# Eleven block units in each of the last two quarters, with the S sums and the den chain moved

## The chip, the cores and the metric

The kernel runs on one core of a Trainium2 chip. The metric is the device time in microseconds of one execution. A core has a matrix engine (TensorE, "PE" in the profile; its weight loads are "PEld"), a vector engine (VectorE, "DVE"), a scalar engine (ScalarE, "ACT"), GpSimd ("POOL"), and a queue engine (SyncE, "SP") that issues most of the transfers. Each engine works through its own list of instructions in order and waits for the others where data or a buffer demands it. TensorE writes into PSUM, which has eight banks of 128 x 512 float32; this kernel cuts the eight banks up by hand.

## The reference

Two branches over the same 2048 tokens of 640 features are blended by a gate.

```python
def _A_ref(x, wqkv, wo):                     # linear attention, 32 heads of 20
    ...
    phi = lambda t: jnp.where(t > 0, t + 1, jnp.exp(t)) + 1e-6
    pq, pk = phi(q), phi(k)
    kv = jnp.einsum("bhsd,bhse->bhde", pk, v)
    z = jnp.einsum("bhsd->bhd", pk)
    num = jnp.einsum("bhqd,bhde->bhqe", pq, kv)
    den = jnp.einsum("bhqd,bhd->bhq", pq, z)[..., None] + 1e-6
    o = num / den
    return (...)(o).reshape(B, S, D) @ wo

def _B_ref(x, w_gate, w_up, w_down):         # 640 -> 1728 -> 640
    return (_gelu(x @ w_gate) * (x @ w_up)) @ w_down

g = _sigmoid((x * gate_w).sum(-1, keepdims=True))
return g * a + (1 - g) * b
```

## The kernel before

The tokens are cut into four quarters of 512, and each quarter into four tiles of 128 (tile 0 to 15). On TensorE the stages follow one another like this (starts of the matmuls in the trace):

| stage | from, us | what |
|---|---|---|
| start, E(0) | 0 | keys and queries of quarter 0, then gate and up of quarter 0 |
| KQ | 44 | keys and queries of quarters 1 to 3 |
| G | 81 | the product of tokens and keys that kv is made of |
| E(1) | 96.7 | gate and up of quarter 1; beside it KV, M and the sums for the down weights |
| F(0) | 128.5 | down of quarter 0, together with its attention part, and the blend |
| E(2) | 146.6 | gate and up of quarter 2 |
| F(1) | 174.1 | |
| E(3) | 192.4 | |
| F(2) | 219.4 | |
| F(3) | 237.5 | down of quarter 3, and the last rows of the output |

**E(q).** The 1728 hidden features are 13 tiles of 128 ("F tiles", `ft`) and half a tile. For one F tile a *plain unit* does gate and up with five 512-column matmuls each. A *block unit* does the same with a 2x2 block scheme of seven products in place of eight: four blocks of gate and up weights (two k tiles each) against four blocks of x (two k tiles by 256 tokens). Each product is two 256-column matmuls; the fifth k tile stays plain, one 512-column matmul each for gate and up. The scheme needs sums of weights (made once by GpSimd in E(0), kept in DRAM as `stash`, fetched again for each block unit of E(2) and E(3)) and sums of x (`tx`, made by VectorE for each quarter).

```python
    WF = tuple(range(4, 12)) + (2, 3)          # F tiles that have weight sums
    ...
    def unit(q, ft, of=UB, ahead=(0, 0)):      # plain
        ...
            return lambda: nc.tensor.matmul(ps, lhsT=w[:, k, f * P : (f + 1) * P], rhs=xT[q][:, k, :],
                                            start=(k == 0), stop=(k == ND - 1))
    ...
    def unit_b(q, ft, fetch):                  # block: p1 to p7 are the seven products
        ...
        def p5():
            two(ub[:, hi_h], s_(1), tx[0], True)
        def p1():
            two(ub[:, lo_h], wg[:, 0:2, fs], X[:, 0:2, lo_h])
            nc.scalar.copy(out=gb[:, lo_h], in_=ub[:, lo_h])
            nc.scalar.copy(out=cp, in_=ub[:, hi_h])
        ...
        def p3():
            nc.vector.tensor_tensor(out=ub[:, hi_h], in0=ub[:, hi_h], in1=c3, op=ALU.add)
            two(gb[:, hi_h], s_(4), X[:, 2:4, hi_h])
            w_fetch(*fetch)                    # sums of the unit five places on
        def g5():
            mm(gb, wg[:, 4, fs], X[:, 4, :])
        ...
        return [p5, p1], [p6], [p7, p3, g5, p2], [u5, p4]
    ...
    runs = {
        0: blocks([3], 12, range(4, 12), [NF - 1]),
        1: list(range(1, NF)),
        2: blocks([NF - 1, 1, 12], 0, range(2, 12), [None]),
        3: blocks([1, 12], 0, range(2, 12), [NF - 1]),
    }
```

A unit ends with a gelu on ScalarE (`gl`) and a product on VectorE, which empties the bank of the up half (line 250, written to `hb` or `hT`).

**F(q).** Down is a block scheme of the same kind, once for each half `a` of the tiles. It needs sums of the weights (`TS`, "T sums") and of the hidden activations (`SS`, "S sums" s1 to s4, each in three parts: h, p and x). `keep` and `join` empty the banks; `beside` puts other work at that place of the order.

```python
        for a in range(2):
            st = [4 * q + 2 * i + a for i in range(2)]
            beside("F", q, a)
            ...
            product(x, a, 0, 0, 0, 0, 0, 0, True, True)
            c1 = keep("c1", x, 0)                       # ScalarE
            product(b11, a, 0, 0, 1, 0, 1, 0, not a, bool(a))
            ...
            product(x, a, 2, 0, 0, 2, 0, 0, False, True)    # needs s2
            c2 = keep("c2", x, 0)
            product(b22, a, 1, 0, 0, 1, 0, 0, not a, True)  # needs s1
            join(d[:], b22, 0, c2)                      # VectorE, the "d join"
            beside("D", q, a)
            product(x, a, 3, 0, 0, 3, 0, 0, False, True)    # needs s3
            c3 = keep("c3", x, 1)
            product(b12, a, 4, 0, 0, 0, 1, 1, not a, bool(a))   # needs s4
            if not a:
                ...
                join(o[0][:, 0:HALF], b11, 0, c1)       # its bank is x of the next half
            join(o[0][:, HALF:D], b12, 0, d)
            dma(out=out2[st[0] * P : (st[0] + 1) * P, :], in_=o[0][:])
            join(o[1][:, HALF:D], b22, 1, c3)
            product(b21, a, 0, 1, 1, 4, 0, 0, False, True)
            join(o[1][:, 0:HALF], b21, 1, c3)
            dma(out=out2[st[1] * P : (st[1] + 1) * P, :], in_=o[1][:])
```

**The den chain.** For each pair of token tiles: `den_mul` (GpSimd: `prod` = pq x zrep), `den_sum` (VectorE: the sum over a head), `den_rec` (GpSimd: `dtmp`), `den_inv2` (VectorE: reciprocal `rg`), `den_out` (GpSimd: pq x rg), `den_turn` (a transposing transfer into `pqT`, which F(q) reads). `den_inv` is den_sum twice, den_rec and den_inv2. Where each piece stands is fixed by a table; its part around F(0):

```python
        (1, 9): [(phase_S, 0, "h", 0)],
        (1, 10): [(phase_S, 0, "p", 0)],
        (1, 11): [(phase_S, 0, "x", 0)],
        (1, 12): [(den_mul, 4, 5)],
        ("F", 0, 0): [(w_fetch, (2, 2), (2, 3), (2, 4)), (phase_S, 0, "h", 1)],
        ("D", 0, 0): [(phase_S, 0, "p", 1), (phase_S, 0, "x", 1)],
        ("F", 0, 1): [(h_twin, 1), (x_tiles,), (t_sums, 2), (den_inv, 4), (den_mul, 6, 7), (den_out, 4, 5)],
        ("D", 0, 1): [(den_inv, 6), (den_out, 6, 7)],
        (2, 0): [(ring_more,), (w_fetch, (2, 5), (2, 6)), (s_tiles, 1), (den_mul, 8, 9), *s_pool(1, 0)],
```

A key `(q, n)` stands after the unit n of E(q), `("F", q, a)` and `("D", q, a)` at the two `beside` calls above.

Of the kernel before, what the change touches and what calls it, by code (L numbers as in the profile page):

```python
# [9 lines left out]
ALU = mybir.AluOpType  # L10
AX = mybir.AxisListType
FP32 = mybir.dt.float32
# [4 lines left out]
def kernel(  # L17
# [12 lines left out]
    nc = tc.nc  # L30
# [71 lines left out]
    x_sb = [x_all[:, 4 * q : 4 * q + 4, :] for q in range(NQ)]  # L102
    WF = tuple(range(4, 12)) + (2, 3)
    WS = 2 * 4
    ws = [ov.tile([P, 2, WS, P], FP16, name=f"ws{i}", tag="slab_a", bufs=NQ) for i in range(3)]
    ws.append(ov.tile([P, 2, WS, P], FP16, name="ws3", tag="slab_g"))
    pk_q = []
# [162 lines left out]

    ws.append(ew["more"])
    stash = dram.tile([len(WF), P, WS, P], FP16, name="stash")

    def w_sums(i):

        n = 2
# [15 lines left out]

    def t_sums(q):

        def blk(k, j):
            return xT[q][:, 2 * k : 2 * k + 2, j * HT : (j + 1) * HT]

        t1, t2, t3, t4 = ew["tx"]
        for out, a0, a1 in ((t1, blk(0, 1), blk(0, 0)), (t2, blk(1, 1), t1), (t3, blk(1, 1), blk(0, 1)),
                            (t4, blk(1, 0), t2)):  # L300
            sums(out, a0, a1, ALU.subtract)

# [423 lines left out]

    def den_inv2(st):
        rg = work.tile([P, 2, H, 1], FP32, name="rg", bufs=2)
        nc.vector.reciprocal(out=rg[:, :, :, 0], in_=den_at[st, "t"][:])
        dn[st], dn[st + 1] = rg[:, 0], rg[:, 1]  # L730
# [74 lines left out]
    def phase_F(q):  # L805
# [35 lines left out]
        for a in range(2):  # L841
# [53 lines left out]
            dma(out=out2[st[1] * P : (st[1] + 1) * P, :], in_=o[1][:])  # L895

    def blocks(first, ramp, fs, last):
# [61 lines left out]
    with tc.manual_schedule(engines={mybir.EngineType.PE, mybir.EngineType.Activation, mybir.EngineType.DVE}):  # L959
# [12 lines left out]
        (0, 4): [(w_sums, 3)],  # L972
        (0, 6): [(w_sums, 4)],
        ("K", 4): [(x_sums, 3)],
    })
# [33 lines left out]
    def s_tiles(q):  # L1009
        if q == 0:  # L1010
            sw = ov.tile([P, NG * D], FP16, name="sw", tag="slab_w")
            sp = ov.tile([P, ND * D], FP16, name="sp", tag="slab_g")
            SS["3"], SS["4"] = (t[:, 0 : KS * TW].rearrange("p (k n) -> p k n", n=TW) for t in (sw, sp))
            SS["more"] = sp[:, KS * TW : KS * TW + WS // 2 * P].rearrange("p (s c) -> p s c", c=P)
            SS["c1"] = sw[:, KS * TW : KS * TW + 4 * HALF].bitcast(FP32).rearrange("p (s n) -> p s n", n=HALF)
        for i in range(1, 5):
            name = f"s{q}_{i}"
            if q == NQ - 1:
                SS[q, i] = big.tile([P, KS, TW], FP16, name=name, tag="pq" if i < 4 else "xT", bufs=NQ if i < 4 else NQ - 1)
            elif i < 3:  # L1020
                SS[q, i] = ov.tile([P, KS, TW], FP16, name=name, tag="slab_a", bufs=NQ)
            else:
                SS[q, i] = SS[str(i)]

    def t_tiles():
        TS[2] = ov.tile([P, KS, HALF], FP16, name="t2", tag="slab_e")
# [3 lines left out]

    def s_pool(q, a):
        return [(phase_S, q, part, a, (3, 1, 2, 4), nc.gpsimd) for part in "hpx"]

    side.update({
        (1, 1): [(m_part, 0), (t_tiles,), (den_mul, 0, 1, 2, 3)],
        (1, 2): [(m_part, 1), (den_inv, 0), (den_out, 0, 1)],
        (1, 3): [(den_inv, 2), (den_out, 2, 3)],
        (1, 4): [(s_tiles, 0), (h_twin, 0), (phase_T, "h", (1,))],
        (1, 5): [(phase_T, "h", (3, 2))],
        (1, 6): [(phase_T, "x", (1, 3))],  # L1040
        (1, 7): [(phase_T, "h", (4,)), (phase_T, "x", (2, 4))],
        (1, 8): [(phase_T, "p", (1, 2, 3, 4))],
        (1, 9): [(phase_S, 0, "h", 0)],
        (1, 10): [(phase_S, 0, "p", 0)],
        (1, 11): [(phase_S, 0, "x", 0)],
        (1, 12): [(den_mul, 4, 5)],
        ("F", 0, 0): [(w_fetch, (2, 2), (2, 3), (2, 4)), (phase_S, 0, "h", 1)],
        ("D", 0, 0): [(phase_S, 0, "p", 1), (phase_S, 0, "x", 1)],
        ("F", 0, 1): [(h_twin, 1), (x_tiles,), (t_sums, 2), (den_inv, 4), (den_mul, 6, 7), (den_out, 4, 5)],
        ("D", 0, 1): [(den_inv, 6), (den_out, 6, 7)],  # L1050
        (2, 0): [(ring_more,), (w_fetch, (2, 5), (2, 6)), (s_tiles, 1), (den_mul, 8, 9), *s_pool(1, 0)],
        (2, 7): [(den_rec, 8), *s_pool(1, 1)],
        (2, 10): [(den_inv2, 8), (lambda: den_out(8, 9, later=True),)],
        ("F", 1, 0): [(den_turn, 8, 9)],
        ("D", 1, 0): [(t_sums, 3), (lambda: pool_hold(ew["tx"][3][:, 0, 0:1]),), (den_mul, 10, 11)],
        ("F", 1, 1): [(h_twin, 2), (den_inv, 10), (den_mul, 12, 13), (den_out, 10, 11)],
        ("D", 1, 1): [(den_inv, 12), (den_mul, 14, 15), (den_out, 12, 13)],
        (3, 0): [(s_tiles, 2), (den_sum, 14, 0), (den_sum, 14, 1), (den_rec, 14), *s_pool(2, 0)],
        (3, 2): [(den_inv2, 14), (lambda: den_out(14, 15, later=True),), *s_pool(2, 1)],
        (3, 11): [(den_turn, 14, 15)],  # L1060
        ("D", 2, 0): [(s_tiles, 3)],
# [4 lines left out]
    })  # L1066
    for n in range(4):
        side[2, 3 + n] = [(den_sum, 8, n // 2, slice(H // 2 * (n % 2), H // 2 * (n % 2 + 1)))]
# [35 lines left out]
```

## Time and profile before

| | before |
|---|---|
| time, median of 3 | 261.82 us (261.49 to 262.46) |
| span of the profiled execution | 259.3 us |
| matmuls | 1755 |
| TensorE clock granted | full |
| GpSimd busy | 135.2 us (52%) |

A profile line of the timeline gives start, duration, engine, source line, operation, what is written and read, its shape, and how many like instructions are merged in it; in brackets stands idle time ahead of it and what ended it. A line of the waits gives who waited for whom, the sum in us, how often, and the longest. Two things are needed for reading TensorE here. First, the end of a matmul is modelled and overlaps the next one, so that a hole of a few tenths is not always shown as idle; the distance from start to start is the sure measure. Second, a wait is charged to the instruction that released it, which may itself have been ready long before and merely have stood behind others in its engine's list.

### The profile page before, as it was taken

Reading aid. Unit: us, or ns where it says so; the run is one execution under the profiler, and the core shown is the slowest. Engines: PE = TensorE matmul, PEld = TensorE weight load, DVE = VectorE, ACT = ScalarE, POOL = GpSimd, SP = SyncE. Lnnn points to the kernel's source line nnn. Section 1 sums busy time; section 2 is a strip of 40 time slices with the busy share of each in tenths; the row PEclk is TensorE's granted clock in tenths of the full one; section 3 lists DMA queues with packets and bytes.
Section 4 is the critical chain, followed back from the end, with each engine's and each line's share of the span. In section 5 each row is a group of like instructions: output and inputs, shape, how many; then the busy total and the mean of one; then the engine's idle time right before and its main releaser. Section 6 shows DMA issues by size and latency. Waiting matters only on the chain.

```text
span 259.3 us, 4883 instructions
## 1 busy us (share of the span) xinstructions
PE 253.8 (98%) x1755; PEld 160.9 (62%) x1755; DVE 183.7 (71%) x366; ACT 121.8 (47%) x271; POOL 135.2 (52%) x158
## 2 busy tenths in 40 slices
PE   8999999999999999999999999999999999999994
PEld 3655686555556775444466647777666787767672
DVE  0698577778779995679999567784756777268632
ACT  3689677555555234732231147762224876311110
POOL 6109995255550004785000999997799999400000
PEclk9999999999999999999999999999999999999999
DMA  7999999900000029125041157441223531011011
GB/s 234 319 350 237 168 357 263 378 4 0 1 3 0 1 41 317 53 68 109 0 125 51 25 129 216 132 142 26 78 51 83 162 93 22 0 52 53 0 51 52
DMA packets 42164, 28.82 MB, mean 111 GB/s; under 512 B 21532, under 2 KB 40860, under 8 KB 42140
## 3 DMA queue, kind: packets, MB, share of 16 engines
q1 hardware_dynamic: 41698, 28.03, 38.5%
q10 hardware_dynamic: 442, 0.49, 0.6%
q8 instruction: 13, 0.21, 0.4%
q14 instruction: 11, 0.09, 0.1%
HBM read 17.86 MB, written 5.24 MB: 89 GB/s over the span
## 4 chain that ended last, share of the span: by engine, by line
PE 88%; DVE 5%; POOL 2%; DMA 2%; issue 1%; SPq 0%; DVEq 0%
PE banks L320 21%; PE banks L827 20%; PE banks L443 17%; PE banks L240 14%; PE banks L330 7%; PE banks L546 6%; DMA wqk<-in_A_wqkv_dram 2%; PE banks L536 2%; DVE o_out L853 1%; POOL prod L709 1%; POOL pq_93 L744 1%; PE banks L834 1%; DVE den L717 1%; DVE tx L61 1%; DVE hb L250 1%
## 5 line engine op out<-in xcount | busy, mean ns | idle before, releaser
L245 ACT ACTIVATE gl<-banks 128x512 bf16<-128x512 f32 x52 | 31.0, 598 | 31.6 <-PE banks L240 17.1
L462 ACT ACTIVATE phi<-banks 128x512 bf16<-128x512 f32 (+1 forms) x36 | 18.8, 526 | 16.2 <-POOL hold L799 8.9
L250 DVE SCALAR_TENSOR_TENSOR hb<-banks,gl 128x512 bf16<-128x512 f32 x26 | 17.8, 683 | 8.4 <-PE banks L320 2.8
L849 ACT ACTIVATE m_all<-banks,omg_s 128x320 f32<-128x320 f32 x16 | 8.4, 527 | 31.6 <-PE banks L827 31.6
L250 DVE SCALAR_TENSOR_TENSOR hT_152<-banks,gl 128x512 bf16<-128x512 f32 x26 | 17.9, 689 | 7.2 <-PE banks L320 4.8
L724 POOL TENSOR_SCALAR dtmp<-den,en_s 128x32 f32<-128x32 f32 x16 | 4.6, 291 | 24.5 <-DVE den L717 23.5
L320 PEld LDWEIGHTS <-wg 128*128 128x128 bf16 x140 | 13.7, 98 | 5.2
L384 DVE TENSOR_TENSOR banks<-banks,zacc 128x256 f32<-128x256 f32 x28 | 12.1, 431 | 6.0 <-ACT zacc L381 3.8
L240 PE MATMUL banks<-xT_89,wg 128*128 128x512 bf16 x65 | 16.2, 379 | 0.0
L240 PE MATMUL banks<-xT_89,wu 128*128 128x512 bf16 x65 | 16.1, 379 | 0.0
L799 POOL CAST hold<-phi 128x1 f32<-128x1 bf16 x12 | 2.2, 183 | 24.6 <-DVE phi L464 24.6
L853 DVE SCALAR_TENSOR_TENSOR o_out<-banks,omg_s,m_all 128x320 bf16<-128x320 f32 x24 | 12.0, 537 | 3.1 <-PE banks L827 3.1
L853 DVE SCALAR_TENSOR_TENSOR m_all<-banks,omg_s,m_all 128x320 f32<-128x320 f32 x8 | 4.4, 550 | 13.2 <-PE banks L827 13.2
L240 PEld LDWEIGHTS <-wu 128*128 128x128 bf16 x80 | 7.8, 98 | 9.4
L381 ACT COPY zacc<-banks 128x256 f32<-128x256 f32 x28 | 10.4, 370 | 6.6 <-PE banks L320 6.5
L849 ACT ACTIVATE sw<-banks,omg_s 128x320 f32<-128x320 f32 x8 | 4.2, 527 | 19.5 <-PE banks L827 19.5
L240 PEld LDWEIGHTS <-wg 128*128 128x128 bf16 x80 | 7.5, 98 | 8.4 <-issue 0.5
L443 PE MATMUL banks<-wqk,xT_88 128*128 128x512 bf16 (+2 forms) x80 | 12.2, 299 | 0.4 <-DMA wqk<-in_A_wqkv_dram 0.4
L709 POOL TENSOR_TENSOR prod<-pq_92,zrep 128x640 f32<-128x640 bf16 x2 | 2.8, 1408 | 18.6 <-ACT zrep L617 18.6
L717 DVE TENSOR_REDUCE den<-prod 128x32 f32<-128x640 f32 (+1 forms) x16 | 11.2, 726 | 0.7 <-POOL prod L709 0.5
L443 PE MATMUL banks<-wqk,xT_89 128*128 128x512 bf16 (+1 forms) x60 | 11.6, 344 | 0.0
L320 PE MATMUL banks<-tx,wr 128*128 128x256 f16 x64 | 11.6, 273 | 0.0
(291 smaller groups left out, 693.1 us busy)
## 6 DMA issues: line engine op xcount, KB each, us to landing
wr<-stash SPq DMA_DIRECT2D x20, 128.0 KB, 2.7
out_dram<-o_out SPq DMA_DIRECT2D x16, 160.0 KB, 1.8
wd<-in_B_w_down_dram SPq DMA_DIRECT2D x1, 2080.0 KB, 9.0
wr_1729<-stash SPq DMA_DIRECT2D x16, 128.0 KB, 2.1
x_all<-in_A_x_dram SPq DMA_DIRECT2D x3, 640.0 KB, 5.7
wqk<-in_A_wqkv_dram SPq DMA_DIRECT2D x1, 800.0 KB
wg<-in_B_w_gate_dram SPq DMA_DIRECT2D x1, 800.0 KB, 9.1
wu<-in_B_w_up_dram SPq DMA_DIRECT2D x1, 800.0 KB
```

What stands on the lines that cost most here:

```text
L240: nc.tensor.matmul(ps[:, t0 : t0 + tw], lhsT=w[:, dk, ft * P : (ft + 1) * P], rhs=xT[q][:, dk, t0 : t0 + tw], start=(dk == 0), stop=(dk == ...
L245: nc.scalar.activation(out=gl[:], in_=psg[:], func=ACT.Gelu_apprx_tanh)
L250: nc.vector.scalar_tensor_tensor(out=hT_cur[q][:, ft, :], in0=psu[:], scalar=HS, in1=gl[:], op0=ALU.mult, op1=ALU.mult)
L320: nc.tensor.matmul(out, lhsT=lhsT, rhs=rhs, start=start, stop=True, skip_group_check=True)
L330: return lambda: nc.tensor.matmul(ps, lhsT=w[:, k, f * P : (f + 1) * P], rhs=xT[q][:, k, :], start=(k == 0), stop=(k == ND - 1))
L443: nc.tensor.matmul(ps[:, 0 : hi - lo], lhsT=xT[q][:, dk, sl * P : (sl + 1) * P], rhs=wqk[:, dk, lo:hi], start=(dk == 0), stop=(dk == ND - 1),)
L462: nc.scalar.activation(out=e[:, lo:top], in_=ps[:, lo:top], func=ACT.Exp)
L546: nc.tensor.matmul(bank[:, 0:HALF], lhsT=lhsT, rhs=rhs, start=(start and n == 0), stop=(stop and n == NG2 - 1), skip_group_check=True)
L717: nc.vector.tensor_reduce(out=den_at[st][:, i, hs], in_=dn[st + i][:].rearrange("p (h c) -> p h c", c=Dh)[:, hs], axis=AX.X, op=ALU.add)
L827: nc.tensor.matmul(bank[:, 0:HALF], lhsT=lhs(sa, ia, ka * KS + kk, a), rhs=rhs(sb, kb * KS + kk, jb), start=(start and kk == 0), stop=(sto ...
L849: nc.scalar.activation(out=c[:], in_=bank[:, 0:HALF], func=ACT.Copy, scale=omg[i])
L853: nc.vector.scalar_tensor_tensor(out=out, in0=bank[:, 0:HALF], scalar=omg[i], in1=c[:], op0=ALU.mult, op1=ALU.add)
```

## The change

It turns F tile 1 into a block unit in E(2) and E(3), so that eleven F tiles of each are block units; for that, one more set of weight sums is made in E(0). It makes the S sums of F(0) earlier, in one piece for both halves, over E(1), so that F(0) has none beside it. With that, it moves the den chain of tiles 4 to 7 and of 12 to 15 to other places: `den_rec` of a pair comes ahead of the outputs of the pair before, and the reciprocal of tiles 8, 9 and 14, 15 comes in two pieces beside later units. A `hold` on GpSimd keeps the den products of tiles 4 and 5 behind the last S sum. The last row of tiles is stored in two halves, the first as soon as it is ready. The core of the diff:

```diff
-    WF = tuple(range(4, 12)) + (2, 3)
+    WF = tuple(range(4, 12)) + (2, 3, 1)
...
-    ws.append(ov.tile([P, 2, WS, P], FP16, name="ws3", tag="slab_g"))
+    ws3 = ov.tile([P, 3, WS, P], FP16, name="ws3", tag="slab_g")
+    ws.append(ws3[:, 0:2])
...
-    ws.append(ew["more"])
+    ws += [ew["more"], ws3[:, 2:3]]
...
-    def den_inv2(st):
-        rg = work.tile([P, 2, H, 1], FP32, name="rg", bufs=2)
-        nc.vector.reciprocal(out=rg[:, :, :, 0], in_=den_at[st, "t"][:])
+    def den_inv2(st, pair=slice(0, 2)):
+        if (st, "r") not in den_at:
+            den_at[st, "r"] = work.tile([P, 2, H, 1], FP32, name="rg", bufs=2)
+        rg = den_at[st, "r"]
+        nc.vector.reciprocal(out=rg[:, pair, :, 0], in_=den_at[st, "t"][:, pair])
...
+            end = q == NQ - 1 and a
...
             join(o[1][:, HALF:D], b22, 1, c3)
+            row = out2[st[1] * P : (st[1] + 1) * P, :]
+            if end:
+                dma(out=row[:, HALF:D], in_=o[1][:, HALF:D])
             product(b21, a, 0, 1, 1, 4, 0, 0, False, True)
             join(o[1][:, 0:HALF], b21, 1, c3)
-            dma(out=out2[st[1] * P : (st[1] + 1) * P, :], in_=o[1][:])
+            dma(out=row[:, 0:HALF] if end else row, in_=o[1][:, 0:HALF] if end else o[1][:])
...
-        2: blocks([NF - 1, 1, 12], 0, range(2, 12), [None]),
-        3: blocks([1, 12], 0, range(2, 12), [NF - 1]),
+        2: blocks([NF - 1, 12], 0, range(1, 12), [None]),
+        3: blocks([12], 0, range(1, 12), [NF - 1]),
...
+        (0, 7): [(w_sums, 5)],
...
+        ("S", 0): [(s_tiles, 0), (phase_S, 0, "h", None, (1,))],
+        ("S", 1): [(phase_S, 0, "h", None, (2,))],
...
-        (1, 6): [(phase_T, "x", (1, 3))],
+        (1, 6): [(phase_S, 0, "h", None, (3, 4)), (phase_T, "x", (1, 3))],
...
-        (1, 9): [(phase_S, 0, "h", 0)],
-        (1, 10): [(phase_S, 0, "p", 0)],
-        (1, 11): [(phase_S, 0, "x", 0)],
-        (1, 12): [(den_mul, 4, 5)],
-        ("F", 0, 0): [(w_fetch, (2, 2), (2, 3), (2, 4)), (phase_S, 0, "h", 1)],
-        ("D", 0, 0): [(phase_S, 0, "p", 1), (phase_S, 0, "x", 1)],
-        ("F", 0, 1): [(h_twin, 1), (x_tiles,), (t_sums, 2), (den_inv, 4), (den_mul, 6, 7), (den_out, 4, 5)],
-        ("D", 0, 1): [(den_inv, 6), (den_out, 6, 7)],
-        (2, 0): [(ring_more,), (w_fetch, (2, 5), (2, 6)), (s_tiles, 1), (den_mul, 8, 9), *s_pool(1, 0)],
+        (1, 9): [(phase_S, 0, "p")],
+        (1, 10): [(phase_S, 0, "x")],
+        (1, 12): [(lambda: pool_hold(SS[0, 4][:, KS - 1, 0:1]),), (den_mul, 4, 5)],
+        ("F", 0, 0): [(x_tiles,), (t_sums, 2), (w_fetch, (2, 1), (2, 2), (2, 3))],
+        ("D", 0, 0): [(den_inv, 4), (den_mul, 6, 7)],
+        ("F", 0, 1): [(h_twin, 1), (den_sum, 6, 0), (den_sum, 6, 1), (den_rec, 6), (den_out, 4, 5)],
+        ("D", 0, 1): [(den_inv2, 6), (den_out, 6, 7)],
+        (2, 0): [(ring_more,), (w_fetch, (2, 4), (2, 5)), (s_tiles, 1), (den_mul, 8, 9), *s_pool(1, 0)],
...
-        (2, 10): [(den_inv2, 8), (lambda: den_out(8, 9, later=True),)],
+        (2, 9): [(den_inv2, 8, slice(0, 1))],
+        (2, 10): [(den_inv2, 8, slice(1, 2)), (lambda: den_out(8, 9, later=True),)],
...
-        ("F", 1, 1): [(h_twin, 2), (den_inv, 10), (den_mul, 12, 13), (den_out, 10, 11)],
-        ("D", 1, 1): [(den_inv, 12), (den_mul, 14, 15), (den_out, 12, 13)],
-        (3, 0): [(s_tiles, 2), (den_sum, 14, 0), (den_sum, 14, 1), (den_rec, 14), *s_pool(2, 0)],
-        (3, 2): [(den_inv2, 14), (lambda: den_out(14, 15, later=True),), *s_pool(2, 1)],
-        (3, 11): [(den_turn, 14, 15)],
+        ("F", 1, 1): [(h_twin, 2), (den_inv, 10), (den_mul, 12, 13)],
+        ("D", 1, 1): [(den_sum, 12, 0), (den_sum, 12, 1), (den_rec, 12), (den_out, 10, 11), (den_mul, 14, 15)],
+        (3, 0): [(s_tiles, 2), (den_inv2, 12), (den_out, 12, 13), *s_pool(2, 0)],
+        (3, 7): [(den_rec, 14), *s_pool(2, 1)],
+        (3, 9): [(den_inv2, 14, slice(0, 1))],
+        (3, 10): [(den_inv2, 14, slice(1, 2)), (lambda: den_out(14, 15, later=True),)],
+        ("F", 2, 0): [(den_turn, 14, 15)],
...
     with tc.manual_schedule():
+        beside("S", 0)
         phase_E(1, 0)
+        beside("S", 1)
```

More of the change, by code (lines that the diff above doesn't have):

```diff
@@ L269, in phase_E @@
             e_half(q, pgu)
-    ws.append(ew["more"])
+    ws += [ew["more"], ws3[:, 2:3]]
     stash = dram.tile([len(WF), P, WS, P], FP16, name="stash")
     def w_sums(i):
-        n = 2
+        n = len(WF[2 * i : 2 * i + 2])
         f0 = WF[2 * i] * P
@@ L291, in w_stash, with t_sums @@
             dma(out=stash[2 * i + f], in_=ws[i][:, f])
-    def t_sums(q):
+    def t_sums(q, eng=nc.vector):
         def blk(k, j):
@@ L300, in t_sums @@
                             (t4, blk(1, 0), t2)):
-            sums(out, a0, a1, ALU.subtract)
+            sums(out, a0, a1, ALU.subtract, eng)
     def w_fetch(*keys, eng=dma):
@@ L1010, in s_tiles @@
         if q == 0:
-            sw = ov.tile([P, NG * D], FP16, name="sw", tag="slab_w")
             sp = ov.tile([P, ND * D], FP16, name="sp", tag="slab_g")
-            SS["3"], SS["4"] = (t[:, 0 : KS * TW].rearrange("p (k n) -> p k n", n=TW) for t in (sw, sp))
+            SS["4"] = sp[:, 0 : KS * TW].rearrange("p (k n) -> p k n", n=TW)
             SS["more"] = sp[:, KS * TW : KS * TW + WS // 2 * P].rearrange("p (s c) -> p s c", c=P)
-            SS["c1"] = sw[:, KS * TW : KS * TW + 4 * HALF].bitcast(FP32).rearrange("p (s n) -> p s n", n=HALF)
-        for i in range(1, 5):
+        for i in (1, 2, 4) if q == 0 else range(1, 5):
             name = f"s{q}_{i}"
@@ L1023, in s_tiles, with s3_tile @@
                 SS[q, i] = SS[str(i)]
+    def s3_tile():
+        sw = ov.tile([P, NG * D], FP16, name="sw", tag="slab_w")
+        SS["3"] = SS[0, 3] = sw[:, 0 : KS * TW].rearrange("p (k n) -> p k n", n=TW)
+        SS["c1"] = sw[:, KS * TW : KS * TW + 4 * HALF].bitcast(FP32).rearrange("p (s n) -> p s n", n=HALF)
     def t_tiles():
@@ L1029, in m_part, with s_pool @@
         phase_M(((0, 0), (0, 1), (1, 0)) if i == 0 else ((1, 1), (2, 0), (2, 1)))
-    def s_pool(q, a):
-        return [(phase_S, q, part, a, (3, 1, 2, 4), nc.gpsimd) for part in "hpx"]
+    def s_pool(q, a, parts="hpx"):
+        return [(phase_S, q, part, a, (3, 1, 2, 4), nc.gpsimd) for part in parts]
     side.update({
+        ("S", 0): [(s_tiles, 0), (phase_S, 0, "h", None, (1,))],
+        ("S", 1): [(phase_S, 0, "h", None, (2,))],
         (1, 1): [(m_part, 0), (t_tiles,), (den_mul, 0, 1, 2, 3)],
@@ L1037 @@
         (1, 3): [(den_inv, 2), (den_out, 2, 3)],
-        (1, 4): [(s_tiles, 0), (h_twin, 0), (phase_T, "h", (1,))],
+        (1, 4): [(s3_tile,), (h_twin, 0), (phase_T, "h", (1,))],
         (1, 5): [(phase_T, "h", (3, 2))],
-        (1, 6): [(phase_T, "x", (1, 3))],
+        (1, 6): [(phase_S, 0, "h", None, (3, 4)), (phase_T, "x", (1, 3))],
         (1, 7): [(phase_T, "h", (4,)), (phase_T, "x", (2, 4))],
         (1, 8): [(phase_T, "p", (1, 2, 3, 4))],
-        (1, 9): [(phase_S, 0, "h", 0)],
@@ L1066 @@
     })
-    for n in range(4):
-        side[2, 3 + n] = [(den_sum, 8, n // 2, slice(H // 2 * (n % 2), H // 2 * (n % 2 + 1)))]
+    for q, st in ((2, 8), (3, 14)):
+        for n in range(4):
+            side[q, 3 + n] = [(den_sum, st, n // 2, slice(H // 2 * (n % 2), H // 2 * (n % 2 + 1)))]
     with tc.manual_schedule():
+        beside("S", 0)
         phase_E(1, 0)
+        beside("S", 1)
         phase_KV()
```

## The prediction

> **What bounds the kernel now.** I read the page first (busy shares, then the slices, then the chain), after that the waits of TensorE, and last the timelines around each place where TensorE stood still.
>
> ```profile
> PE 253.8 (98%) x1755; PEld 160.9 (62%) x1755; DVE 183.7 (71%) x366; ACT 121.8 (47%) x271; POOL 135.2 (52%) x158
> ...
> PE 88%; DVE 5%; POOL 2%; DMA 2%; issue 1%; SPq 0%; DVEq 0%
> ```
>
> TensorE is the bound from end to end: busy 98% of 259.3 us, at full clock. A shorter time needs fewer streamed columns on TensorE, fewer holes between its matmuls, or a shorter head or tail. The chain leaves TensorE (the 5% DVE and 2% POOL) mainly from 129.87 to 149.79, inside the first down stage F(0). The waits that the profile counts for TensorE are only these:
>
> ```profile
> PE banks L206 <- PEq L1088: 0.8, 1, 0.8
> PE banks L443 <- DMA wqk<-in_A_wqkv_dram: 0.4, 1, 0.4
> PE banks L330 <- DVE o_out L853: 0.4, 1, 0.4
> ```
>
> The first two belong to the start, which the change leaves alone. The third is at the seam F(0) to E(2). Because a matmul's end is modelled, I look at starts instead. A 320-column matmul starts about 0.136 us after the one before it, a 512-column one 0.216 us after.
>
> ```profile
> 137.38 0.57 PE L827 MATMUL banks<-hb,pqT_1312 128*128 128x320 f16 x3
> 138.07 0.30 PE L827 MATMUL banks<-wd,hT_152 128*128 128x320 bf16 x1
> ...
> 147.71 1.67 PE L330 MATMUL banks<-xT_90,wg 128*128 128x512 bf16 x7
> 149.79 1.24 PE L330 MATMUL banks<-xT_90,wu 128*128 128x512 bf16 x5 [0.41 <-DVE o_out L853]
> ```
>
> Three matmuls from 137.38 make the next start due at 137.38 + 3 x 0.136 = 137.79; it came at 138.07, 0.28 late. Seven from 147.71 make it due at 149.22; it came at 149.79, 0.57 late. Both waits are for a PSUM bank that VectorE has yet to empty. Why VectorE is late is seen in its own timeline and GpSimd's:
>
> ```profile
> 137.34 0.22 DVE L61 TENSOR_TENSOR sp<-pqT_1312,s_2_1358 128x128 f16<-128x128 bf16 x1
> 137.48 0.54 DVE L853 SCALAR_TENSOR_TENSOR o_out<-banks,omg_s,sw 128x320 bf16<-128x320 f32 x1
> ...
> 148.81 0.55 DVE L729 RECIPROCAL rg<-dtmp 128x64 f32<-128x64 f32 x1 [2.40 <-POOL dtmp L724]
> 149.28 1.37 DVE L853 SCALAR_TENSOR_TENSOR o_out<-banks,omg_s,m_all 128x320 bf16<-128x320 f32 x3
> ```
>
> ```profile
> 145.51 2.50 POOL L744 TENSOR_TENSOR pq_93<-pq_93,rg 128x640 bf16<-128x640 bf16 x2
> 148.11 0.67 POOL L724 TENSOR_SCALAR dtmp<-den,en_s 128x32 f32<-128x32 f32 x2
> ```
>
> At 137.48 the join that frees the bank stands behind VectorE's S sums of the second half (from 132.93). At 149.28 the three joins stand behind a reciprocal that waited 2.40 us for `dtmp`, and `dtmp` stood in GpSimd's queue behind two products of tiles 4 and 5 (145.51). Nothing was slow; the queues had the wrong order.
>
> **What the Trainium skill says.** "TensorE: Matmul & The Clock Gate", section "Wait — 56ns, not 53.3ns?", gives a warm start-to-start step of N/2.4 + about 2.5 ns. The trace agrees: five 512-column matmuls take 1.08 us (151.95 to 153.03, 216 ns each), two 256-column ones 0.22 us (154.11 to 154.33). "SBUF — State Buffer", section "Who interferes with whom", says that a VectorE instruction with two SBUF inputs contends with a GpSimd one that reads SBUF. This trace agrees: the same 128x1920 subtraction takes 2.36 us at 116.94 while GpSimd is busy with `prod`, and 1.14 us at 121.51 when GpSimd is idle.
>
> **The change, part by part.**
>
> *Block units.* F tile 1 becomes a block unit in E(2) and E(3). A plain unit is 10 x 512 = 5120 columns; a block unit is 14 x 256 + 2 x 512 = 4608. By the steps above, 10 x 0.216 = 2.16 us against 14 x 0.109 + 2 x 0.216 = 1.96 us: 0.20 each, all of it on TensorE's path: **-0.40 us**. It adds four GpSimd sums of half the usual size in E(0) (the full size takes 1.15, so about 2.6 us in all). GpSimd's last such sum ends at 42.14 and its next work starts at 48.52, so that is free. It also adds a 128 KB store and two fetches of 256 KB.
>
> *S sums of F(0) in one piece.* VectorE does s1 beside G, s2 beside E(1), s3 and s4 beside unit 6, p and x parts later, and none in F(0). That takes the 4.1 us from 132.93 to 137.48 (less one join) off VectorE in F(0). The d join, run at 135.17, may then start when its bank is complete, about 133.5. The two den sums (0.74 each), `dtmp` and the reciprocal now come between it and the freeing join; in the old order first sum to end of reciprocal is 140.78 to 143.2, 2.4 us. So the join is possible at about 136.5, and its own products end near 136.7. It ends near 137.3, before 137.79: **-0.28 us**.
>
> *Den chain.* `dtmp` of tiles 6 and 7 now stands ahead of the outputs of 4 and 5 on GpSimd, and its products start some 7 us sooner (behind the hold on the last S sum, near 129). The last reciprocal of F(0) has its input by 141, and the joins run as their banks complete: **-0.57 us**. The seam F(1) to E(3) has the same form in small (matmul start at 194.00, 0.06 late) and loses its reciprocal too. Near 171.2 and 172.8 two more starts are 0.10 and 0.12 late while a whole reciprocal sits in VectorE's queue (169.94); it is split in two there. I count **-0.10** for all of these.
>
> *Last row in halves.* The end is
>
> ```profile
> 255.58 0.55 DVE L853 SCALAR_TENSOR_TENSOR o_out<-banks,omg_s,m_all 128x320 bf16<-128x320 f32 x1 [0.21 <-PE banks L827]
> 256.16 0.33 SPq L895 DMA_DIRECT2D out_dram<-o_out  x1
> ```
>
> and 3.1 us from that issue to the span's end. Half of the 160 KB now leaves earlier, beside the last nine matmuls. At the page's best slice rate of 378 GB/s, 80 KB take 0.21 us; the rest of the 3.1 us stays, as "SBUF — State Buffer", section "The DMA setup-cost knee", has it: a fixed part of about 2 us whatever the size (no row here measures that part alone). The earlier half is issued after the row before it (254.94 + 0.33) and before 256.16, so it doesn't push the last one back. **-0.20 us** as an estimate.
>
> Sum: -0.40 - 0.28 - 0.57 - 0.10 - 0.20 = -1.55, so 260.27 from 261.82. I add about 0.1 for a small new wait somewhere, and say **260.4 us**.
>
> **Rivals.** *VectorE falls behind in E(1).* It is busy 20.8 of 22.8 us there. Two sums of 128x1536 come in at unit 6: from 0.47 us a step for 768 elements and 1.07 for 1920, about 0.87 each, 1.75 together. Against it: GpSimd no longer works beside them, so the 2.36 us subtraction should come down to 1.14 and the 0.93 one (119.83) to about 0.3, 1.8 us back. F(0)'s first bank is the one unit 9 leaves by 126.1 and TensorE wants it at 128.47; even the whole 1.75 fits. If it didn't, I would expect up to 1 us of new holes from 122 to 129, and about 261.
>
> *kvt comes late.* s1 pushes G's last joins from 97.4 to at most 98.3 (KV matmuls start at 98.95), and s2 pushes the three kvt products from 101.2 to about 101.9; M's matmuls start at 102.47. About 0.6 us remain each time. If VectorE loses more, a hole of some tenths opens there: 260.7.
>
> *A fetch starves a block unit.* The queue of fetches is in order, with the transposes of tiles 12 and 13 ahead of E(3)'s last fetches. The waits of the DMA queue list 8.4 us behind GpSimd for this quarter's transposes (`pq_630`). I put the issue near 199.5 and the landing (2.7 us) near 202; the block that needs it starts near 204 in the new count. If the wait is real, up to 2 us come back: 261 to 262.
>
> *Only the columns count.* If another entry of those queues takes the place of the two removed waits, only 0.6 us remain: 261.2.
>
> **Range and chances.** The sum of parts with every gain is 1.55 us; without the two bank waits it is 0.7; the three runs before spread by 1.0 us. I take 259.6 to 261.4 for 8 in 10. A 2% move would be 5.2 us, over three times the sum of all parts, so within 2% has a chance of 0.97, faster 0.02, slower 0.01.
>
> **What would show it.** Right: TensorE with 1767 matmuls; the start after the 137.38 group and the one after the 147.71 group in step with those before them; VectorE free of S sums in F(0); E(2) and E(3) shorter by about 0.2 us each. Wrong: a wait of TensorE on `kvt`, on `wr` from the stash or on VectorE's `hb` or `s_` tiles, or a last store that takes as long from its issue to the end as before.

## The result and the profile after

| | before | after |
|---|---|---|
| time, median | 261.73 us (261.49 to 262.46, 4 runs) | 259.48 us (259.09 to 259.76, 4 runs) |
| ratio after / before | | 0.9908, 95% interval 0.9884 to 0.9932 |
| span of the profiled execution | 259.3 us | 257.8 us |
| matmuls | 1755 | 1767 |

The gain is 2.25 us where 1.42 was predicted, and the time lies 0.1 us under the predicted range. From the page of the changed kernel, the busy times and the shares of the chain:

```profile
PE 253.9 (98%) x1767; PEld 162.5 (63%) x1767; DVE 182.2 (71%) x362; ACT 123.8 (48%) x277; POOL 136.2 (53%) x163
...
PE 97%; DMA 1%; DVE 0%; issue 0%
```

Of the waits of TensorE that were shown for the kernel before, the changed one lists only that of the start:

```profile
PE banks L207 <- PEq L1106: 0.8, 1, 0.8
```

The two bank waits are gone. In TensorE's timeline the group that follows the 137.38 group of before, and the first gate and up after the 147.71 group, now come in step:

```profile
137.78 0.57 PE L830 MATMUL banks<-hb,pqT_1322 128*128 128x320 f16 x3
138.19 0.98 PE L830 MATMUL banks<-wd,hT_152 128*128 128x320 bf16 x6
...
147.82 1.24 PE L331 MATMUL banks<-xT_90,wg 128*128 128x512 bf16 x5
148.90 0.38 PE L321 MATMUL banks<-tx,wr 128*128 128x256 f16 x2
```

Three 320-column matmuls from 137.78 take 0.41 us, five 512-column ones from 147.82 take 1.08. The reason stands in VectorE's timeline, whose reciprocal of tiles 6 and 7 no longer waits for anything and is done well ahead of the joins of E(2)'s seam:

```profile
137.28 0.45 DVE L856 SCALAR_TENSOR_TENSOR o_out<-banks,omg_s,sw 128x320 bf16<-128x320 f32 x1
...
143.81 0.54 DVE L732 RECIPROCAL rg<-dtmp 128x64 f32<-128x64 f32 x1
145.72 1.01 DVE L856 SCALAR_TENSOR_TENSOR o_out<-banks,omg_s,m_all 128x320 bf16<-128x320 f32 x2 [1.37 <-PE banks L830]
```

From start to start, F(0) went from 18.16 to 17.87 us (-0.29), E(2) with F(1) from 45.80 to 44.94 (-0.86), E(3) with F(2) from 45.08 to 45.07. That E(3) gained nothing is a hole of 0.23 us for a slot of weight sums fetched from the stash:

```profile
204.28 0.38 PE L321 MATMUL banks<-tx,wu 128*128 128x256 f16 x2
204.73 0.61 PE L321 MATMUL banks<-tx,wr 128*128 128x256 f16 x4
```

Two 256-column matmuls from 204.28 make the next start due at 204.50; it came at 204.73. The end is shorter by more than half a microsecond:

```profile
254.82 0.55 DVE L856 SCALAR_TENSOR_TENSOR o_out<-banks,omg_s,m_all 128x320 bf16<-128x320 f32 x1 [0.21 <-PE banks L830]
...
255.40 0.33 SPq L902 DMA_DIRECT2D out_dram<-o_out  x1
```

From the issue of the last store to the end of the span it is now 2.43 us, 3.13 before.

### The profile page after: what moved, and what is told of

It reads as the page before. It is cut to its first block, busy times and chain, and to the rows that moved or that the text cites. A ratio compares the mean times of both kernels' runs of the same rounds, so it can differ in the third digit from the quotient of the medians.

```text
span 257.8 us, 4930 instructions
## 1 busy us (share of the span) xinstructions
PE 253.9 (98%) x1767; PEld 162.5 (63%) x1767; DVE 182.2 (71%) x362; ACT 123.8 (48%) x277; POOL 136.2 (53%) x163
## 4 chain that ended last, share of the span: by engine, by line
PE 97%; DMA 1%; DVE 0%; issue 0%
PE banks L830 27%; PE banks L321 21%; PE banks L444 17%; PE banks L241 14%; PE banks L331 6%; PE banks L547 6%; PE banks L537 2%; DMA wr<-stash 1%; PE banks L207 1%; PE banks L837 1%; PE banks L232 1%; PE banks L678 0%; PE banks L647 0%; DVE o_out L856 0%; PE banks L617 0%
## 5 line engine op out<-in xcount | busy, mean ns | idle before, releaser
L321 PEld LDWEIGHTS <-wg 128*128 128x128 bf16 x150 | 14.7, 98 | 5.5
L385 DVE TENSOR_TENSOR banks<-banks,zacc 128x256 f32<-128x256 f32 x30 | 12.8, 427 | 5.9 <-ACT zacc L382 4.8
L382 ACT COPY zacc<-banks 128x256 f32<-128x256 f32 x30 | 11.1, 370 | 7.3 <-PE banks L321 7.3
L321 PE MATMUL banks<-tx,wr 128*128 128x256 f16 x76 | 14.0, 273 | 0.1
L241 PEld LDWEIGHTS <-wu 128*128 128x128 bf16 x80 | 7.8, 98 | 9.4
L444 PE MATMUL banks<-wqk,xT_88 128*128 128x512 bf16 (+2 forms) x80 | 12.9, 314 | 0.0
L241 PEld LDWEIGHTS <-wg 128*128 128x128 bf16 x80 | 7.5, 98 | 8.4 <-issue 0.5
L373 ACT COPY banks<-banks 128x256 f32<-128x256 f32 x30 | 10.7, 357 | 2.7
L321 PEld LDWEIGHTS <-wu 128*128 128x128 bf16 x90 | 8.8, 98 | 4.5
```

Of the source, the lines that this page charges most:

```text
L241: nc.tensor.matmul(ps[:, t0 : t0 + tw], lhsT=w[:, dk, ft * P : (ft + 1) * P], rhs=xT[q][:, dk, t0 : t0 + tw], start=(dk == 0), stop=(dk == ...
L321: nc.tensor.matmul(out, lhsT=lhsT, rhs=rhs, start=start, stop=True, skip_group_check=True)
L444: nc.tensor.matmul(ps[:, 0 : hi - lo], lhsT=xT[q][:, dk, sl * P : (sl + 1) * P], rhs=wqk[:, dk, lo:hi], start=(dk == 0), stop=(dk == ND - 1),)
```

## The experiments

To compare executions I cut each span in three: up to the first columns of E(0) (the first matmul on `xT` and `wg`), from there to the start of the last matmul on `m_all` in F(3) (the *stretch*), and the *tail* from there to the end. Every number is from the trace of that execution, in us; "last landing" is the end of the last packet of the last store (its semaphore is complete some 0.35 us later), and "slot" is the time for which TensorE stood still for a fetched slot of weight sums.

| kernel | columns from | stretch | slot in E(2) | tail | last landing to end |
|---|---|---|---|---|---|
| before | 14.37 | 239.65 | 0 | 5.27 | 1.73 |
| before again (b1, b2, b3) | 14.59, 14.88, 14.61 | 240.83, 240.83, 239.68 | 1.12, 1.13, 0 | 5.26, 5.27, 5.27 | 1.72, 1.72, 1.73 |
| blocks alone (e1) | 14.83 | 241.80 | 1.44 | 4.79 | 1.25 |
| S sums and den chain alone (e2) | 14.14 | 238.64 | 0 | 5.25 | 1.70 |
| halves alone (e3) | 14.47 | 239.66 | 0 | 5.14 | 1.78 |
| before, six more transfers (e4) | 14.45 | 239.98 | 0.30 | 4.74 | 1.20 |
| after | 14.77 | 238.49 | 0 | 4.57 | 1.21 |
| after again (a1) | 14.96 | 238.25 | 0 | 4.57 | 1.21 |
| after, late turn of 12 and 13 (e8) | 13.99 | 238.25 | 0 | 4.57 | 1.21 |
| after, late turns of 4 to 7 (e10) | 14.77 | 242.86 | 2.68 | 4.56 | 1.21 |
| after, two more transfers (e5) | 15.45 | 239.01 | 0 | 4.73 | 1.37 |
| after, last row in one store (e7) | 14.67 | 238.25 | 0 | 4.80 | 1.25 |

The first column differs with the loads at the start, which no edit but those of e4 and e5 touches, and I leave it out. So the change is -1.16 us in the stretch in its first profiled execution, -1.40 in the second, and -0.70 in the tail.

Further executions have a span and a time, but no timeline. The spans of 64 of before run from 259.2 to 262.3 us with a median of 259.95, so the one behind the prediction, 259.3, is among the shortest. Seven of the changed kernel, the two in the table among them, run from 256.9 to 258.0. The time outside the span is 1.7 to 1.8 us in most executions, but in 18 of those 64 it is above 1.85, up to 3.25, and it was 2.5 in the one behind the prediction, which is why its time still looked like the median. In the 51 executions of kernels with 1767 matmuls it is never above 1.84. By the means that is 0.15 us in favour of the change (1.89 against 1.74), by the medians 0.01. What brings it is not shown.

**The parts one by one.** My first theory, A, was that the surplus came from the end of the program: the new transfers of the blocks put the last store on another DMA queue, for which SyncE waits last. The rival, B, gave it to the parts themselves. Blocks alone (e1): the change's block lines and nothing else.

```diff
-    WF = tuple(range(4, 12)) + (2, 3)
+    WF = tuple(range(4, 12)) + (2, 3, 1)
...
-        2: blocks([NF - 1, 1, 12], 0, range(2, 12), [None]),
-        3: blocks([1, 12], 0, range(2, 12), [NF - 1]),
+        2: blocks([NF - 1, 12], 0, range(1, 12), [None]),
+        3: blocks([12], 0, range(1, 12), [NF - 1]),
```

> The kernel before with the block units alone (F tile 1 as a block unit in E(2) and E(3), with its weight sums, store and fetches). Theory A (the parts work as predicted, and the rest of the gain is the end of the program): span 0.40 us shorter by the fewer columns, less up to 0.25 given back in E(3) by a fetch that lands late. Beside that the end changes for reasons that have nothing to do with the blocks: five more transfers put the last store on another semaphore of the list that SyncE waits through at the end, now the fourth of five waits and no longer the second, about 0.4 us less; and 24 more TensorE instructions move the fetches of instructions, so that the time outside the span falls from 2.5 to about 1.75 us. In all about -1.4 us. Theory B (the predicted parts were too small, the end does not matter): the blocks alone give -0.4 to -0.6 us in time and in span.

Measured 263.07 us, ratio 1.006 (1.0043 to 1.0076): slower, as neither theory had it (the time outside the span did fall, to 1.68 to 1.79 us). TensorE's waits say why:

```profile
PE banks L321 <- DMA wr<-stash: 1.3, 1, 1.3
PE banks L321 <- DVE o_out L854: 1.2, 2, 0.8
```

By starts, the fetched slot costs 1.44 us in E(2) and another 0.21 in E(3), and the bank waits at the two seams grow from 0.57 to 1.00 and from 0.06 to 0.50; it is now the first matmul of a block unit that waits there, and no longer one of a plain unit. Less 0.40 for the columns that makes 2.1 us more, and the stretch is longer by 2.15. The tail, 0.48 shorter, takes part of it back. The first expectation is in both theories too simple: the blocks need the rest of the change.

The S sums and the den chain alone (e2), with the change's lines for `phase_S`, `s3_tile`, `den_inv2` and the table, ten block units kept:

```diff
-        ("D", 0, 0): [(phase_S, 0, "p", 1), (phase_S, 0, "x", 1)],
+        ("D", 0, 0): [(den_inv, 4), (den_mul, 6, 7)],
...
-        ("D", 0, 1): [(den_inv, 6), (den_out, 6, 7)],
+        ("D", 0, 1): [(den_inv2, 6), (den_out, 6, 7)],
```

> The changed kernel with ten block units and the last row in one store again: the S sums and the den chain alone. Theory A: the two bank waits of F(0) and E(2) (0.28 and 0.57 us) and the small holes (0.1) go, -0.9 us in time and in span; the end is as before, since the number of transfers and of TensorE instructions is as before. Theory B: this part carries the surplus, -1.6 us.

Measured 260.37 us, ratio 0.9956 (0.9939 to 0.9972). The stretch is 1.01 us shorter, close to the sum of 0.95 that the prediction had for these steps. By the medians, 261.86 of before in this comparison, the gain is 1.49; what the other half microsecond is, the repetitions of before show further down.

The last row in halves alone (e3):

```diff
+            if end:
+                dma(out=row[:, HALF:D], in_=o[1][:, HALF:D])
...
-            dma(out=out2[st[1] * P : (st[1] + 1) * P, :], in_=o[1][:])
+            dma(out=row[:, 0:HALF] if end else row, in_=o[1][:, 0:HALF] if end else o[1][:])
```

> The kernel before with the last row stored in halves alone. Theory A: the store lands 0.17 us sooner after its issue, but one more transfer puts it on the semaphore that SyncE waits for first at the end, so the four waits after it come on top: between -0.2 and +0.2 us. Theory B (the halves themselves shorten the end): -0.7 us, as the end of the changed kernel is 0.74 us shorter from the last join to the end of the span.

Measured 261.35 us, ratio 0.9985 (0.9964 to 1.0006), which the times can't tell from no change. The trace can: the last store lands 1.22 us after its issue, 1.40 before, and the tail is 0.13 shorter. The halves do not bring the 0.7 us.

The kernel before with the x loads of quarters 1 to 3 cut, six transfers more (e4):

```diff
-    for q in (1, 2, 3):
-        dma(out=x_sb[q][:], in_=x_view[:, 4 * q : 4 * q + 4, :])
+    for q, cuts in ((1, (0, 1, 2, 4)), (2, (0, 1, 2, 4)), (3, (0, 1, 2, 4))):
+        for lo, hi in zip(cuts, cuts[1:]):
+            dma(out=x_sb[q][:, lo:hi], in_=x_view[:, 4 * q + lo : 4 * q + hi, :])
```

> The kernel before with the loads of the x rows of quarters 1 to 3 cut into three transfers each: the same bytes, six more transfers, far from any wait of TensorE. Theory A: the last store now has the semaphore that SyncE waits for last, so the end after its landing shrinks from 1.39 us to about 0.85 us: -0.5 us in span and time. Theory B: no change, within 0.2 us.

Measured 261.75 us, ratio 0.9999 (0.9975 to 1.0024): no gain in time. Yet the trace has the shorter tail, 4.74 against 5.27, with nothing changed near the end of the program. What hides it is in the stretch: 0.30 us for a slot due at 157.45, which the first profile of before had not shown.

**What the end is made of.** Two edits to the changed kernel. With two more transfers near the start (e5, as e4 but for quarter 1 alone), the last store is back in second place of SyncE's list of five waits:

> The changed kernel with one edit: two of the x loads near the start are cut, two transfers more in all, so that the last row's second half is on another DMA queue, one whose semaphore SyncE waits for early in its list at the end of the program. Theory A (the end of the changed kernel is half a us shorter because its last store is on the queue that is waited for last): from the last landing to the end of the span 1.7 us instead of 1.2, the time 0.5 us longer, 260.0 us. Theory B (the shorter end comes from the store in halves itself): 1.2 us as before, 259.5 us.

Measured 259.16 us, ratio 0.9898 (0.9867 to 0.9928). From the last landing to the end it is 1.37 us, between the two theories. (Its stretch is longer than in the second execution of the changed kernel by 0.59 us in KQ, for which the trace shows no single cause, and by 0.16 for a slot in E(3).) The last row in one store again (e7, the edit of e3 taken back):

> The changed kernel with one edit: the last row is stored in one transfer again. Theory A (halves make the store land 0.17 us earlier; the remaining 0.5 us of the shorter end are the place of its queue in the list of waits, which this edit moves by one place): the tail from the last join's start to the end of the span is longer by 0.2 to 0.5 us, the time 259.7 to 260.0 us. Theory B (the halves bring the whole 0.7 us at the end): 260.2 us. Theory C (the end costs nothing in either form): 259.5 us.

Measured 259.59 us, ratio 0.9904 (0.9875 to 0.9933), the tail longer by 0.23, of which 0.18 is the landing: theory A in the tail, at the lower end of its numbers, while the time is below what it said. The times of both can't be told from the changed kernel's; the traces can be. Here are SyncE's semaphore waits at the end of the program: durations in ns (least, median, longest), then the first and the last start. Before:

```profile
L1099 SPq EVENT_SEMAPHORE  x5: 27/28/1322, 256.5 to 258.4; - x5
L1099 SPq DRAIN  x1: 13/13/13, 258.5 to 258.5; - x1
```

After:

```profile
L1117 SPq EVENT_SEMAPHORE  x5: 28/28/28, 255.8 to 257.0; - x5
L1117 SPq DRAIN  x1: 13/13/13, 257.1 to 257.1; - x1
```

The changed kernel with two more transfers:

```profile
L1118 SPq EVENT_SEMAPHORE  x5: 28/28/1165, 257.0 to 258.4; - x5
L1118 SPq DRAIN  x1: 13/13/13, 258.4 to 258.4; - x1
```

In before the second of the five (the one of 1322 ns) waits for the last store and is over at 257.93, and the drain comes at 258.52, 0.59 us later. In e5 it is also the second, over at 258.20, and the drain comes at 258.42, 0.22 later. In after the last store is waited for last, and the drain comes 0.04 later. Each wait that stands behind the last store costs 0.06 us, so three of them 0.19. The rest of before's 0.59 is a pause of 0.36 between its third and fourth wait. Such a pause of 0.35 to 0.36 us, with the awaited transfers long landed, is there in all six executions of before, e2 and e3, and in none of the others. So the 0.52 us by which landing to end fell are about 0.16 for the place in the list and 0.36 for that pause; what makes the pause stays open.

**The late slot.** To see whether the block units hang on the early transposes, the changed kernel with one edit, the transposes of tiles 4 to 7 issued after the row stores (e10):

```diff
-        ("D", 0, 1): [(den_inv2, 6), (den_out, 6, 7)],
-        (2, 0): [(ring_more,), (w_fetch, (2, 4), (2, 5)), ...],
+        ("D", 0, 1): [(den_inv2, 6), (lambda: den_out(6, 7, later=True),)],
+        (2, 0): [(den_turn, 4, 5, 6, 7), (ring_more,), (w_fetch, (2, 4), (2, 5)), ...],
```

(`den_out` of tiles 4 and 5 in F(0) is made `later` in the same way.)

> The changed kernel with one edit: the DMA transposes of tiles 4 to 7 are issued at the start of quarter 2, after the row stores, as late as they landed in the kernel before; the sums, the reciprocals and the GpSimd products stay where they are. Theory A (the eleventh block unit of quarter 2 is only paid for because the den chain of the change brings the transposes forward: the fetches of the later weight slots wait for the transposes, both in the queue and because the slots lie in the memory that the transposes read): a wait for a fetched weight slot of 1 to 3 us opens at about 154.8 us, and the time is 260.5 to 262.5 us. Theory B (the change's gain in quarter 2 comes from VectorE's earlier work alone, and the 1.44 us wait of the blocks alone has another cause): no such wait, 259.5 us.

Measured 263.61 us, ratio 1.0051 (1.0031 to 1.007): theory A's wait, and a longer time than it said. The slower kernel waits where it should:

```profile
PE banks L321 <- DMA wr<-stash: 2.8, 2, 2.5
```

Every engine but SyncE has the same list of instructions as in the changed kernel, so the 4 us come from this one place in SyncE's queue. They are not all waiting. The trace has TensorE's clock at half from 156.99 to 160.41 us, from shortly before the end of the wait. The clock row of the page (40 slices of the span, in tenths), and the busy times of the engines from 157.00 to 160.40, where 0.50 is the granted clock:

```profile
PEclk9999999999999999999999997999999999999999
157.00:160.40 3.40, 2.75 (x13) 1.91 (x15) 0.86 (x2) 1.02 (x3) 3.09 (x7) 0.50 0.74 232
```

Four 256-column matmuls from 157.42 take 0.83 us there, and 4 x 0.109 = 0.44 at the full clock. Half the clock for 3.42 us loses 1.71; with the wait of 2.68 and another 0.24 in E(3) that makes the 4.6 us by which the stretch is longer than 238.25. The other executions divide likewise: the 7 of 19 with a mean granted clock of 0.998 or more take 261.75 to 262.56 us, inside theory A's range, and the 12 with 0.992 to 0.994 take 263.06 to 265.08. After the shorter waits of e1 (1.44 us) and of b1 and b2 below (1.12 and 1.13) the clock stays full.

SyncE's own timeline, before:

```profile
146.81 6.66 SPq L751 DMA_TRANSPOSE pqT_1622<-pq_93  x4
153.57 0.53 SPq L891 DMA_DIRECT2D out_dram<-o_out  x1
154.19 0.38 SPq L895 DMA_DIRECT2D out_dram<-o_out  x1
154.91 1.75 SPq L314 DMA_DIRECT2D wr_1729<-stash  x4
```

and after:

```profile
142.32 5.92 SPq L754 DMA_TRANSPOSE pqT_1623<-pq_93  x4
148.34 0.70 SPq L895 DMA_DIRECT2D out_dram<-o_out  x1
149.13 0.38 SPq L902 DMA_DIRECT2D out_dram<-o_out  x1
150.41 1.76 SPq L315 DMA_DIRECT2D wr_1724<-stash  x4
```

The first of these fetches lands 2.1 us after its issue in both (its semaphore is complete): at 157.00 before and at 152.47 after. TensorE wants it at 157.37 before and at 154.76 after:

```profile
157.37 0.38 PE L320 MATMUL banks<-tx,wr_1729 128*128 128x256 f16 x2
154.76 0.38 PE L321 MATMUL banks<-tx,wr_1724 128*128 128x256 f16 x2
```

The kernel before thus has 0.37 us to spare, the changed one 2.3. In e1 the block units come earlier and the fetch later (155.44), and the 0.37 turn into a wait.

So near the edge, one profile may not be the rule. Three more executions of the kernel before:

> The kernel before, unchanged: another execution of it under the profiler. Its runs in the first two rows of experiments had a median span of 260.0 us and up to 261.7, while its first profile has 259.3. Theory A (the first profile caught an execution in which the fifth weight slot of quarter 2 landed just in time; in others TensorE waits for it): some of these looks show a wait of 0.2 to 1.5 us for a fetched slot at 157.4 us, and the stretch from the first columns to the last join is longer than 239.65 us by that. Theory B (the longer spans come from the loads at the start): the stretch is 239.65 us within 0.1 in every look, and the first columns start later than 14.4 us.

> As for the first repetition of the kernel before: theory A, a wait for a fetched slot at 157.4 us in some looks; theory B, none, and a later start.

> As for the first repetition of the kernel before: theory A, a wait for a fetched slot at 157.4 us in some looks; theory B, none, and a later start.

Two of the three wait (times 262.39, 262.82 and, without the wait, 261.54 us). TensorE in the first of them, first its waits, then its timeline:

```profile
PE banks L320 <- DMA wr<-stash: 1.0, 1, 1.0
```

```profile
157.17 0.60 PE L320 MATMUL banks<-xT,wg 128*128 128x512 bf16 x3
158.73 0.61 PE L320 MATMUL banks<-tx,wr 128*128 128x256 f16 x4 [0.96 <-DMA wr<-stash]
```

The second line was due at 157.60. The slot came 1.49 us later than in the first profile when counted from the start of E(2), which used up the 0.37 to spare and left 1.12. SyncE shows where a third of that comes from. One of its four transposes took 1.87 us,

```profile
L751 SPq DMA_TRANSPOSE pqT<-pq x4: 1227/1228/1867, 147.0 to 152.9; - x4
```

against 1.41 at most in the first profile, and the fetch was issued at 155.61, 0.47 us later by that count. The rest is its landing, 3.1 us after the issue and not 2.1. The second of the three is alike (1.82 and 3.1). Theory A holds. Theory B does not explain these two: the stretch lengthens, though their first columns are 0.2 and 0.5 us later as well.

The changed kernel once more (a1):

> The changed kernel, unchanged: another execution under the profiler, timed beside the kernel before. Theory A (the change took the slots' landing off the edge): the stretch from the first columns to the last join is 238.5 us within 0.1, as in its first profile, with no wait in quarter 2, and its times spread less than those of the kernel before. Theory B: the stretch is the same too, but the times spread as those before do. Time 259.5 us by both.

Measured 259.46 us, ratio 0.9867 (0.9797 to 0.9936). Its stretch is 238.25, without the 0.23 us of the first execution, a little more than the 0.1 that I had allowed, and with no wait in E(2). The medians here and of the next experiment include one execution each at a lower granted clock (268.4 us at 0.95, and 262.74 at 0.992), which the ratios leave out. The three others are too few to say that its times spread less.

**A version that goes on from there.** The changed kernel with the turn of tiles 12 and 13 put behind the fetches of E(3) (e8):

```diff
-        (3, 0): [(s_tiles, 2), (den_inv2, 12), (den_out, 12, 13), *s_pool(2, 0)],
+        (3, 0): [(s_tiles, 2), (den_inv2, 12), (lambda: den_out(12, 13, later=True),), *s_pool(2, 0)],
...
+        (3, 8): [(den_turn, 12, 13)],
```

> The changed kernel with one edit: the DMA transposes of tiles 12 and 13 are issued after quarter 3's block units have begun (beside unit 8) instead of before its weight fetches. Theory A (the 0.23 us wait for a fetched weight slot at 204.7 us comes from two transposes, 2.5 us long, that stand ahead of the fetches in SyncE's queue): the wait is gone, quarter 3's columns and the F stage after them last 44.85 us instead of 45.07, and the time is 259.3 us, 0.2 under the changed kernel's 259.5. Theory B (the fetch waits for its slot in the ring, not for the queue): the wait stays, 259.5 us. Against both: the later transposes make down's third quarter late, and the time rises.

SyncE's queue in the changed kernel:

```profile
197.25 2.52 SPq L754 DMA_TRANSPOSE pqT_2307<-pq_635  x2
199.87 1.48 SPq L315 DMA_DIRECT2D wr<-stash  x3
```

and with the late turn, where the same fetches leave 4.5 us sooner:

```profile
195.42 2.11 SPq L315 DMA_DIRECT2D wr<-stash  x3
...
206.93 2.53 SPq L754 DMA_TRANSPOSE pqT<-pq  x2
```

The wait is gone and the stretch 238.25 us. Measured 258.87 us, ratio to before 0.988 (0.9851 to 0.9909), the lowest median of all. Since the second execution of the changed kernel had no such wait either, what e8 removes is a wait that comes in some executions; its interval overlaps the changed kernel's, and that it is faster is not shown.

## Why the prediction was wrong, point by point

- *What bounds the kernel.* Right about TensorE, and wrong in one sentence: "The waits that the profile counts for TensorE are only these". That was true of the one execution I read. A fourth wait, 1.12 to 1.13 us for a fetched slot in E(2), is there in two of four executions of the kernel before; over these four and e3 and e4, whose block units and den chain are the same, its mean is (0 + 1.12 + 1.13 + 0 + 0 + 0.30) / 6 = 0.43 us, an estimate from few executions. It fits the spans: their median for before lies 0.65 us above the span that I reckoned from. Moving the den chain takes the wait away: none of the six executions of e2, e5, e7, e8 and the changed kernel has it, and e10, with the late transposes, has it again. This is the first failed step.
- *Block units, -0.40.* Right, where no slot comes late: e2 to the second execution of the changed kernel is 238.64 to 238.25, -0.39. With the wait in E(3) it is -0.15. And it holds only together with the den chain: alone they lengthen the stretch by 2.15. (The added store is 256 KB, as the others to the stash are, and not 128; nothing rests on it.)
- *S sums, -0.28.* Right: F(0) is 0.29 shorter and its start in step.
- *Den chain, -0.57 and -0.10.* Right in size: E(2) with F(1) lost 0.86, of which 0.20 is its block unit, so 0.66. Of the smaller holes those near 171.2 (0.10) and at 194.00 (0.06) are gone; the one of 0.12, now before 172.08, is still there, though its reciprocal is split.
- *Last row in halves, -0.20.* The store lands 0.18 sooner (e7), as reckoned. The failed step is "the rest of the 3.1 us stays". It rested on "SBUF — State Buffer", section "The DMA setup-cost knee", whose fixed part of about 2 us bears on the transfer alone. Here the transfer takes less, 1.75 us before and 1.58 after from issue to the complete semaphore (1.40 and 1.22 to the last packet), and from the last packet to the end of the span lies a stretch of 1.73 us that fell to 1.21, by the place of the last store in SyncE's list and by the pause. Neither was meant by the change and the prediction has neither, so these 0.52 us of the gain are luck. The whole tail lost 0.70.
- *Rivals.* VectorE does not fall behind in E(1), and `kvt` isn't late. "A fetch starves a block unit" came true in E(3) with 0.23 us in one of two executions, not with 2; I looked for it only where the change might bring it, and not where it took it away.
- *The sum.* Stretch -1.28 (mean of the two executions, against the first of before), slot -0.43, tail -0.70: -2.41, against a measured 2.25 with an interval of 1.8 to 3.0. The first columns and the time outside the span are left out; their differences (0.25 us later and 0.15 less by the means) are of the size of what does not close. The prediction's own terms without the two failed steps come to -1.35 in the stretch, close to -1.28; that the allowance of 0.1 for a new wait is near the mean wait of 0.12 in E(3) is chance. The miss of 0.83 is 0.50 in the tail and about 0.43 for the slot, less small change.

## What to carry to other kernels

A list of waits from one execution has only what waited in that execution: where a transfer lands a few tenths before its use, look at its slack, and at a second profile, before reckoning what a change can bring. When one part of a change brings more users for a queue and another clears that queue, judge them together: here the blocks alone cost 1.2 us and, beside the earlier transposes, bring 0.4. A wait of TensorE can cost more than its length: in e10 one of 2.7 us came with a loss of 1.7 us by the halved clock. Under half a microsecond, read each stage by start to start and the end by the list of waits, since the times did not separate such edits.

## What was not expected of the hardware

- The end of the program costs by position: 0.06 us for each of SyncE's waits behind that for the last store. The pause of 0.35 to 0.36 us in that list is followed within 0.6 to 0.8 us by an 8 KB transfer on the queue that the page calls "instruction", in all six executions that have it; in the eight that lack it no 8 KB one comes within 9 us of the end. That SyncE stood waiting for instructions is likely by this, but no run shows it as the cause.
- The same 128 KB fetch at the same place landed in 2.0 to 2.1 us (before, b3, e3), 2.4 (e4) or 3.1 us (b1, b2). In the last two an instruction transfer of 8 KB ran beside it for 0.87 and 0.83 us, and for 0.31 to 0.70 in the first three. In b1 and b2 fifteen of the sixteen increments of the fetch's semaphore are there by 157.67 and 157.93, and the last comes 1.0 us later, so it is one part of the transfer that was held up. By what stays open.
- SyncE's waits hold up what stands behind them. In e10 the last transpose was issued by 153.57 and the fetch behind it at 155.14: its slot lies in memory that the transposes read. "DMA: Bandwidth & Descriptors", section "Anatomy of one DMA — SWDGE (gpsimd) path", says, of transfers that GpSimd issues, that the transfer engines don't wait on semaphores and the issuing sequencer does. The trace agrees for SyncE: in these 1.57 us it issues nothing and has two waits, for the four transposes' semaphores among others.
